# Attention with a threshold and a low-rank mixer on one core: the instruction order made by a list scheduler, u formed in row order, the threshold on ScalarE

## The chip, the core and the metric

The kernel runs on one core of a Trainium2 chip. The core has five instruction streams that run side by side and wait for each other by semaphores: TensorE (PE, matmuls and transposes, results to PSUM), VectorE (DVE), ScalarE (ACT), GpSimd (POOL, here the casts of weights and most of the DMA issues) and SyncE (SP, here the DMA transposes). Each takes its instructions strictly in the order in which the program lists them, so the order is part of the kernel. The metric is the device time of one execution in microseconds, lower is better. A "profile" is one execution taken by the hardware profiler, and its "span" reaches from the first to the last instruction.

## The reference

Eight batches of eight heads, sequence 576, head size 64. Attention keeps only the scores within tau = 0.02 of the row's maximum. Its output, 576 x 512 per batch, goes through a mixer: a low-rank mixing along the sequence (rank 32), a sum, and a two-layer network of width 2048. All inputs and the output are float32.

```python
scores = scale * np.matmul(q, k.transpose(0, 1, 3, 2))
thresh = np.max(scores, axis=-1, keepdims=True) - tau
scores = np.where(scores >= thresh, scores, -1000000000.0)
scores = scores - np.max(scores, axis=-1, keepdims=True)
attn = np.exp(scores)
attn = attn / (np.sum(attn, axis=-1, keepdims=True) + 1e-09)
x = np.matmul(attn, v)            # heads side by side: (batch, 576, 512)
xt = x.transpose(0, 2, 1)
h = xt @ U @ V
u = x + h.transpose(0, 2, 1)
ch = np.maximum(u @ w_ch1, 0.0) @ w_ch2
return (u + ch).astype(np.float32)
```

## The kernel before

Work is cut into 32 head pairs (`hp`, four to a batch `b`) and each pair into five score steps (`i`): four of 128 query rows with both heads apart (`x` = 0, 1), and a fifth of 64 rows that holds both heads in one tile. There are 160 steps and 288 score tiles of 128 x 576.

One step: TensorE forms the scores of a tile from `qT` and `kT` (lines 250 and 258, float32, into `scores`, which is held once). DVE copies them to `s_sb` with their sign turned and takes the row's minimum `m` (`weigh`, L267). ACT takes the exponential (`exponential`, L275). DVE adds tau to `m` (`threshold`, L282) and then zeroes what lies below the threshold and sums the row (`select`, L289, into one of eight `w_ring` buffers). SP transposes the weights by DMA into `wT` (L294, L297).

A pair's other work, in its order: its q and k are turned by TensorE (`prepare_qk`, L214 and two tails of 64 columns at L215) and copied by ACT with the scale on q (L222 to L231); v is split into two bf16 parts; the weights are multiplied with v (`mm`, L315, 40 matmuls) and copied out; the result is turned back to rows (`back`, L340 to L345) and divided by the row sums (`scale_rows`, L348, L353), which is x; a bf16 copy (`narrow`, L365) is multiplied with U (`low_rank`, L375) and gives `tt`, 32 rows. Then `turn` forms u transposed in one go: float32 transposes of x and, accumulated on them in the same PSUM bank, the product of `tt` and V (L390 to L395). ACT copies that to bf16 as `uT`.

When the fourth pair of a batch has its `uT`, its mixer units are put on a queue (`mixer_units`): 32 units of four matmuls with W1 and a relu (L415, L421), then units of eight matmuls with W2 (L437) for each 128 rows of output, the last of which adds the product of V and `tt` (L441, L445), since the output is u + ch and x alone is at hand in row order. DVE adds x (L450), POOL sends the rows (L454 to L458). The four loose PSUM banks are handed out by `bank1`.

The order is written out in one loop over pairs and steps. In pass `p` the scores of pair `p` run beside the preparation of pair `p + 1` (in step 1), the weighting of pair `p - 1` (step 2), its back and low rank (steps 3 and 4) and the turn of pair `p - 2` (step 0). Mixer units fill in by a fixed credit per step (`share`, L502). In the first six passes matmuls on a zero tile (`fill`, L470) keep TensorE's clock up. Weights are loaded by POOL, one piece a step from the second pair on.

Of the kernel before, what the change touches and what calls it, by code (L numbers as in the profile page):

```python
# [8 lines left out]
P = 128  # L9
# [7 lines left out]
DM = H * D  # L17
# [5 lines left out]
NPAIR = H // 2  # L23

# [5 lines left out]
def rows(i):  # L30
    return P if i < 4 else HB


@with_exitstack
def kernel(
# [22 lines left out]
    make_identity(nc, ident)  # L58

# [29 lines left out]
    ttpool = pool("tt", 4)  # L89
    upool = pool("uT", 2)  # L90
    opool = pool("o", 3)
# [7 lines left out]
    last = [0, 0, 0, 0]  # L99
    held = [False] * 4  # L100
    clock = [0]
    sums = []

    def bank1():

        while all(held):
            sums.pop(0)()
        n = min((n for n in range(4) if not held[n]), key=lambda n: last[n])
        held[n] = True
        return bank[n], n  # L110

    def free(*ns):

        for n in ns:
            clock[0] += 1
            last[n] = clock[0]
            held[n] = False

    def load_pair(src, b, hp, name, engine):
        raw = rawpool.tile([P, NT, 2, D], FP32, name=name, tag=name)  # L120
        sv = src[b, 2 * hp:2 * hp + 2].rearrange("j (p t) d -> p t j d", p=HB)
        for j in range(2):
            engine.dma_start(raw[0:HB, :, j, :], sv[:, 0:NT, j, :])  # L123
            engine.dma_start(raw[HB:P, 0:4, j, :], sv[:, NT:9, j, :])  # L124
        return raw

    def weight_units():

        def u():
# [5 lines left out]
        def vv():  # L135
# [8 lines left out]
        def w1(t, h):  # L144
# [3 lines left out]
        def w2(c):  # L148
# [4 lines left out]
        return ([u, vv] + [lambda t=t, h=h: w1(t, h) for h in range(2) for t in range(4)]  # L153
                + [lambda c=c: w2(c) for c in range(8)])

    def build_v(raw):

        vh = vpool.tile([P, NT, 2, 2, D], BF16, name="vh", tag="vh")
        for part, ts in ((P, slice(0, 4)), (HB, slice(4, 5))):
            src = raw[0:part, ts, :, :]  # L160
            hi = vh[0:part, ts, 0, :, :]
            nc.scalar.copy(out=hi, in_=src)  # L162
            nc.gpsimd.tensor_tensor(out=vh[0:part, ts, 1, :, :], in0=src, in1=hi,  # L163
                                    op=ALU.subtract)
        return vh

    ring = [0]

    class Batch:
# [3 lines left out]
        def __init__(self, b, before):  # L173
            self.b = b
            self.odd = b % 2
            self.h4 = slice(HB * self.odd, HB * self.odd + HB)

            self.main = slice(HB * self.odd, HB * self.odd + 512)
            self.rest = slice(0, HB) if self.odd else slice(512, S)
            self.even = before  # L180

        def start(self):

            self.x = xpool.tile([P, 4, DM], FP32, name="x", tag="x")
            self.tt = ttpool.tile([R, DM], BF16, name="tt", tag="tt")
            self.uT = upool.tile([P, 4, S], BF16, name="uT", tag="uT")
            if self.odd:
                self.x4 = self.even.x4
            else:
                self.x4 = x4pool.tile([P, DM], FP32, name="x4", tag="x4")  # L190

    class Pair:


        def __init__(self, b, hp):
            self.b, self.hp = b, hp

        def load(self, eq=None, ek=None):
            self.qraw = load_pair(q, self.b, self.hp, "qraw", eq or nc.gpsimd)
            self.kraw = load_pair(k, self.b, self.hp, "kraw", ek or nc.gpsimd)  # L200
            self.vraw = load_pair(v, self.b, self.hp, "vraw", nc.gpsimd)

        def prepare_qk(self):

            tails, t_ = bank1()
            copies = []
            out = []
            for x, raw in enumerate((self.qraw, self.kraw)):  # L210
                tT = qkpool.tile([P, S], FP32, name="qkT", tag="kT" if x else "qT")
                ps, n = bank1()
                for t in range(4):
                    nc.tensor.transpose(ps[:, t * P:(t + 1) * P], raw[:, t, :, :], ident)  # L214
                nc.tensor.transpose(tails[:, x * HB:(x + 1) * HB], raw[0:HB, 4, :, :],  # L215
                                    ident[0:HB, 0:HB])
                out.append(tT)
                copies.append((ps, n))
            self.qT, self.kT = out

            def q_main():
                nc.scalar.mul(out=out[0][:, 0:512], in_=copies[0][0], mul=-scale)  # L222
                free(copies[0][1])

            def k_main():
                nc.scalar.copy(out=out[1][:, 0:512], in_=copies[1][0])
                free(copies[1][1])

            def rest():
                nc.scalar.mul(out=out[0][:, 512:S], in_=tails[:, 0:HB], mul=-scale)  # L230
                nc.scalar.copy(out=out[1][:, 512:S], in_=tails[:, HB:P])  # L231
                free(t_)

            return q_main, k_main, rest

        def prepare_v(self):
            self.vh = build_v(self.vraw)

        def start(self):
            self.wT = wtpool.tile([P, NT, 2, S], BF16, name="wT", tag="wT")  # L240
            self.den = d_ring[(self.b * NPAIR + self.hp) % 4]

        def scores(self, i):

            if i < 4:
                sct = pair_bank
                for c in range(2):
                    for j in range(2):
                        hs = slice(64 * j, 64 * j + 64)
                        nc.tensor.matmul(sct[j][:, c, 0:HC], self.qT[hs, i * P:(i + 1) * P],  # L250
                                         self.kT[hs, c * HC:(c + 1) * HC], start=True, stop=True)
            else:
                one = pair_bank[0]
                sct = [one]
                for c in range(2):
                    for j in range(2):
                        hs = slice(64 * j, 64 * j + 64)
                        nc.tensor.matmul(one[hs, c, 0:HC], self.qT[hs, 512:S],  # L258
                                         self.kT[hs, c * HC:(c + 1) * HC], start=True, stop=True)
            self.sct = sct  # L260
            self.m = small.tile([P, 2], FP32, name="m", tag="m")
            self.ssb, self.esb = [], []

        def weigh(self, i, x):

            s_sb = spool.tile([P, S], FP32, name="s_sb", tag="s_sb")
            nc.vector.tensor_scalar(  # L267
                out=s_sb.rearrange("p (a c) -> p a c", a=2), in0=self.sct[x][:, :, 0:HC],
                scalar1=0.0, scalar2=None, op0=ALU.add, op1=ALU.min,
                accum_out=self.m[:, x:x + 1])  # L270
            self.ssb.append(s_sb)

        def exponential(self, x):
            e_sb = epool.tile([P, S], BF16, name="e_sb", tag="e_sb")
            nc.scalar.activation(out=e_sb, in_=self.ssb[x], func=ACT.Exp,  # L275
                                 bias=self.m[:, x:x + 1], scale=-1.0)
            self.esb.append(e_sb)

        def threshold(self):
            n = len(self.sct)  # L280
            self.thr = small.tile([P, 2], FP32, name="thr", tag="thr")
            nc.vector.tensor_scalar(out=self.thr[:, 0:n], in0=self.m[:, 0:n], scalar1=tau_f,  # L282
                                    scalar2=None, op0=ALU.add)

        def select(self, i, x):

            w_sb = w_ring[ring[0] % NW]
            ring[0] += 1
            nc.vector.scalar_tensor_tensor(  # L289
                out=w_sb[:, 0:S], in0=self.ssb[x], scalar=self.thr[:, x:x + 1],  # L290
# [324 lines left out]
```

## Time and profile before

| what | us |
|---|---|
| median of 3 runs | 752.41 |
| lowest and highest run | 750.87, 755.83 |
| the profiled execution's own time | 751.19 |
| its span | 749.4 |

The page of the profile gives the busy time of each engine, and a query by window gives the same for any stretch. A matmul's end is modelled and matmuls overlap in the array, so the lengths of matmuls that follow each other sum to more than the time they take; the starts are exact. In rows of groups, "idle before" is the engine's idle time just ahead of these instructions and what ended it. A DMA share of 1 means that the core's 16 DMA engines are busy all the time.

### The profile page before, as it was taken

The page shows a single profiled execution, that of the slowest core. Times are in us where ns is not written, and L with a number is a line of the kernel's source. Part 1 is how long each engine was busy: PE and PEld are TensorE (multiplying, and loading weights), DVE is VectorE, ACT ScalarE, POOL GpSimd, SP SyncE. Part 2 cuts the span into 40 slices and gives each one's busy share as a digit, 9 for nine tenths or more (in the row PEclk, how much of TensorE's full clock was granted, in tenths as well). Part 3 has the DMA queues.
Part 4 walks back from the last instruction along what each step waited for, and adds up shares of the span by engine and source line. Part 5 has one row for each costly group of instructions (what it writes and reads, how often), then busy time and mean ns, then how long its engine had stood idle before and what let it go on. Part 6 is the DMA issues. An engine that isn't in the chain of part 4 may idle for free.

```text
span 749.4 us, 15084 instructions
## 1 busy us (share of the span) xinstructions
PE 710.8 (95%) x5119; PEld 422.0 (56%) x5162; DVE 523.3 (70%) x1489; ACT 434.7 (58%) x961; POOL 380.2 (51%) x589
## 2 busy tenths in 40 slices
PE   9887789999999999999999999999999999999995
PEld 4454456665566555664566555665566555665562
DVE  4887487767977788667877778777877677778101
ACT  4565267755677455775577545774577555774340
POOL 9776555465655345554573456543664565310102
PEclk9998799999999999999999999999999999999998
DMA  6999997776974586766786686766886666545202
GB/s 123 165 136 185 158 183 133 109 116 109 178 133 99 107 132 150 121 106 102 136 150 109 116 149 119 132 98 103 147 146 114 115 140 124 100 75 85 52 15 56
DMA packets 220701, 90.30 MB, mean 120 GB/s; under 512 B 206208, under 2 KB 211264, under 8 KB 220624
## 3 DMA queue, kind: packets, MB, share of 16 engines
q1 hardware_dynamic: 195776, 47.52, 43.8%
q0 software_dynamic: 23632, 41.51, 26.8%
q8 instruction: 41, 0.67, 0.4%
q10 hardware_dynamic: 1216, 0.30, 0.2%
q14 instruction: 36, 0.29, 0.1%
HBM read 36.86 MB, written 9.44 MB: 62 GB/s over the span
## 4 chain that ended last, share of the span: by engine, by line
PE 77%; DVE 10%; ACT 5%; issue 3%; DMA 3%; POOL 1%; DVEq 0%; SPq 0%; POOLq 0%; ACTq 0%
PE bank L437 16%; PE scores L250 16%; PE bank L415 16%; PE bank L315 10%; DVE s_sb L267 5%; PE scores L258 4%; DVE w_ring L289 4%; PE bank L214 3%; ACT e_sb L275 3%; PE bank L390 2%; DMA wT<-w_ring 2%; PE bank L375 2%; PE bank L474 1%; PE bank L441 1%; PE bank L392 1%
## 5 line engine op out<-in xcount | busy, mean ns | idle before, releaser
L275 ACT ACTIVATE e_sb<-s_sb,m 128x576 bf16<-128x576 f32 x288 | 218.3, 775 | 131.3 <-DVE s_sb L267 87.5
L267 DVE TENSOR_SCALAR_CACHE_REDUCE s_sb<-scores 128x576 f32<-128x576 f32 x288 | 208.3, 748 | 103.8 <-PE scores L250 99.3
L289 DVE SCALAR_TENSOR_TENSOR w_ring<-s_sb,thr,e_sb 128x576 bf16<-128x576 f32 x288 | 230.9, 822 | 58.0 <-ACT e_sb L275 50.1
L250 PE MATMUL scores<-qkT 64*128 64x288 f32 x1024 | 167.7, 433 | 7.9 <-DVE s_sb L267 7.4
L163 POOL TENSOR_TENSOR vh<-vraw,vh 128x512 bf16<-128x512 f32 x64 | 55.7, 889 | 208.6 <-ACT vh L162 208.6
L415 PE MATMUL bank<-uT,W1b 128*128 128x288 bf16 x1024 | 145.8, 286 | 7.3 <-ACT R L421 6.8
L437 PE MATMUL bank<-W2b,R 128*128 128x512 bf16 x544 | 131.4, 380 | 3.4 <-issue 2.5
L250 PEld LDWEIGHTS scores<-qkT 64*128 64x128 f32 x1024 | 93.5, 187 | 53.4 <-issue 16.3
L415 PEld LDWEIGHTS <-W1b 128*128 128x128 bf16 x1024 | 94.0, 97 | 47.5 <-issue 21.4
L421 ACT ACTIVATE R<-bank 128x288 bf16<-128x288 f32 x256 | 97.3, 409 | 6.9 <-PE bank L415 1.4
L315 PE MATMUL bank<-wT,vh 128*64 128x288 bf16 (+1 forms) x1280 | 91.4, 292 | 5.8 <-DMA wT<-w_ring 5.6
L437 PEld LDWEIGHTS <-R 128*128 128x128 bf16 x576 | 51.7, 98 | 66.0 <-issue 12.0
L315 PEld LDWEIGHTS <-vh 128*64 128x64 bf16 (+1 forms) x1280 | 68.0, 111 | 32.0 <-issue 23.5
L398 ACT CAST uT<-bank 128x512 bf16<-128x512 f32 x32 | 18.7, 585 | 69.6 <-PE bank L392 69.6
L454 POOL DMA_DIRECT2D out_dram<-o x32 | 17.9, 558 | 72.7 <-DVE o L450 70.9
L450 DVE TENSOR_TENSOR o<-bank,x 128x512 f32<-128x512 f32 x36 | 24.8, 690 | 37.1 <-issue 21.2
L123 POOL DMA_DIRECT2D vraw<-in_v_dram x64 | 46.1, 721 | 2.7 <-issue 2.1
L222 ACT ACTIVATE qkT<-bank 128x512 f32<-128x512 f32 x32 | 19.1, 597 | 45.8 <-PE bank L214 45.8
L123 POOL DMA_DIRECT2D qraw<-in_q_dram x62 | 43.9, 707 | 3.4 <-issue 2.5
L123 POOL DMA_DIRECT2D kraw<-in_k_dram x62 | 43.9, 708 | 1.3 <-DMA W1b<-in_moe_w_ch_dram 0.8
L124 POOL DMA_DIRECT2D vraw<-in_v_dram x64 | 42.9, 671 | 1.2 <-DMA qraw<-in_q_dram 1.2
L124 POOL DMA_DIRECT2D kraw<-in_k_dram x62 | 40.9, 660 | 2.4 <-DMA W1b<-in_moe_w_ch_dram 2.4
(73 smaller groups left out, 701.7 us busy)
## 6 DMA issues: line engine op xcount, KB each, us to landing
out_dram<-o POOLq DMA_DIRECT2D x72, 128.0 KB, 3.0
vraw<-in_v_dram POOLq DMA_DIRECT2D x64, 80.0 KB, 4.0
wT<-w_ring SPq DMA_TRANSPOSE x320, 3.9
qraw<-in_q_dram POOLq DMA_DIRECT2D x62, 80.0 KB, 2.7
kraw<-in_k_dram POOLq DMA_DIRECT2D x62, 80.0 KB, 3.8
vraw<-in_v_dram POOLq DMA_DIRECT2D x64, 64.0 KB, 4.1
qraw<-in_q_dram POOLq DMA_DIRECT2D x62, 64.0 KB, 2.8
kraw<-in_k_dram POOLq DMA_DIRECT2D x62, 64.0 KB, 3.7
```

The source lines that it names most:

```text
L123: engine.dma_start(raw[0:HB, :, j, :], sv[:, 0:NT, j, :])
L124: engine.dma_start(raw[HB:P, 0:4, j, :], sv[:, NT:9, j, :])
L163: nc.gpsimd.tensor_tensor(out=vh[0:part, ts, 1, :, :], in0=src, in1=hi, op=ALU.subtract)
L250: nc.tensor.matmul(sct[j][:, c, 0:HC], self.qT[hs, i * P:(i + 1) * P], self.kT[hs, c * HC:(c + 1) * HC], start=True, stop=True)
L258: nc.tensor.matmul(one[hs, c, 0:HC], self.qT[hs, 512:S], self.kT[hs, c * HC:(c + 1) * HC], start=True, stop=True)
L267: nc.vector.tensor_scalar(out=s_sb.rearrange("p (a c) -> p a c", a=2), in0=self.sct[x][:, :, 0:HC], scalar1=0.0, scalar2=None, op0=ALU.add ...
L275: nc.scalar.activation(out=e_sb, in_=self.ssb[x], func=ACT.Exp, bias=self.m[:, x:x + 1], scale=-1.0)
L289: nc.vector.scalar_tensor_tensor(out=w_sb[:, 0:S], in0=self.ssb[x], scalar=self.thr[:, x:x + 1], in1=self.esb[x], op0=ALU.is_le, op1=ALU.mult,
L315: nc.tensor.matmul(self.av[c][64 * j:64 * j + 64, 0:HC], self.vh[0:nk, kt, part, j, :], self.wT[0:nk, kt, j, c * HC:(c + 1) * HC], start=( ...
L415: nc.tensor.matmul(ps[:, 0:HC], W1b[:, dt, ft * P:(ft + 1) * P], bt.uT[:, dt, c * HC:(c + 1) * HC], start=(dt == 0), stop=(dt == 3))
L421: nc.scalar.activation(out=R2[:, ft, lo:lo + HC], in_=ps[:, 0:HC], func=ACT.Relu)
L437: nc.tensor.matmul(ch, R2[:, ft, lo:lo + P], W2b[:, ft, :], start=(ft == 0), stop=False)
```

## The change

The loop is replaced by a list of tasks with a model. Every piece of work becomes a `Task`: an engine, an assumed cost, the tasks it depends on, the PSUM banks it takes or frees, and a rank. `Order.run` keeps a clock for each of the five engines and each bank. It repeatedly takes, for each engine, the tasks that could start within 0.15 us of the first that can, picks the lowest rank among them, and lists the earliest of the five picks. A task's end reaches other engines after a fixed delay (`SIGNAL`). Where the model sees TensorE idle for over 0.45 us, it lists fillers of 0.22 us. Mixer tasks have a due step (`when`): before it they rank last, from it on first. The 24 fillers at the very start stand outside of the model's clock.

```diff
+    SIGNAL = (0.25, 0.18, 0.15, 0.2, 0.1)
...
+        def rank(c):
+            s, t = c
+            if t.when is not None:
+                return (t.when - 1000.0 if t.when <= steps + (1.0 if t.kind == kind else 0.0) else t.when + 1000000.0, s)
+            return (t.ready + t.off, s)
...
+                first = min(s for s, _ in cands)
+                s, t = min((c for c in cands if c[0] <= first + 0.15), key=rank)
+                if best is None or s < best[0]:
+                    best = (s, t)
...
+                while at[PE] + 0.45 < s and last[n] <= at[PE]:
+                    self.filler(n)
+                    at[PE] += 0.22
...
+        due = NT * NPAIR * (b + 1) + 9
...
+                t = add(PE, 0.52, up, uT + weights1 + freed, banks=1, kind="p1",
+                        when=due + 10 * c + 10 * ft / 16)
...
+    for _ in range(24):
+        fill(0)
+    order.run()
```

The computation changes in four places. The threshold moves from DVE to ACT. q and k are loaded into one tile `qkraw`, so that their tails lie side by side and are turned by one transpose and copied once; the scale moves from the copy of q into `weigh`. The weighting is two tasks, one for each half of the columns, with the same 40 matmuls.

```diff
-            nc.vector.tensor_scalar(out=self.thr[:, 0:n], in0=self.m[:, 0:n], scalar1=tau_f,
-                                    scalar2=None, op0=ALU.add)
...
+            nc.scalar.activation(out=st["thr"][:, 0:nx], in_=st["m"][:, 0:nx], func=ACT.Identity,
+                                 bias=tau_t[:, 0:1], scale=1.0)
...
+            nc.tensor.transpose(bank[t.got[0]][:, 0:P], pr.qkraw[:, 4, :, :], ident)
```

And u is formed in row order. `spread` multiplies V and `tt` into rows, DVE adds that to x in place (`sum_u`), ACT makes a bf16 copy `ub`, and TensorE turns the copy in bf16. The tail rows of a batch are done once, with its last pair. The output then adds u from the tile, and the matmuls with V at the end of each output tile go.

```diff
-            for i in range(4):
-                nc.tensor.matmul(ups[:, i * P:(i + 1) * P], bt.x[:, i, cols], ident,
-                                 is_transpose=True, start=(i == 0), stop=False)
-            nc.tensor.matmul(ups, bt.tt[:, cols], Vb[:, 0:512], start=False, stop=True)
...
-                            nc.tensor.matmul(ch, Vb[:, i * P:(i + 1) * P], bt.tt, start=False,
-                                             stop=True)
...
+            for i in range(4):
+                nc.tensor.matmul(bank[t.got[0]][:, i * P:(i + 1) * P], Vb[:, i * P:(i + 1) * P],
+                                 bt.tt[:, pr.cols], start=True, stop=True)
+            if last:
+                nc.tensor.matmul(bank[t.got[1]][bt.h4, :], Vb[:, 512:S], bt.tt, start=True,
+                                 stop=True)
...
+            nc.vector.tensor_add(out=bt.x[:, :, pr.cols],
+                                 in0=bank[h.got[0]].rearrange("p (t m) -> p t m", t=4),
+                                 in1=bt.x[:, :, pr.cols])
...
+            nc.scalar.copy(out=pr.ub, in_=bt.x[:, :, pr.cols])
...
+            ps = bank[t.got[0]][:, 0:256].bitcast(BF16)
+            for i in range(4):
+                nc.tensor.transpose(ps[:, i * P:(i + 1) * P], pr.ub[:, i, :], identb)
```

Three places show how instructions now stand. The first is the start of TensorE's list. Before, 24 fillers (L474) stand ahead of the first transposes of q and k:

```order
L474 LDWEIGHTS idle
L474 MATMUL bank_143<-idle 128x512
L214 MATMUL bank_145<-ident,qraw 128x128 x4
L215 MATMUL bank_144<-ident,qraw 128x64
L214 MATMUL bank_146<-ident,kraw 128x128 x4
L215 MATMUL bank_144<-ident,kraw 128x64
L250 MATMUL scores_141<-qkT 128x288
```

Now the transposes are those of lines 311 and 326, and fillers (L215) stand on both sides of them:

```order
L215 LDWEIGHTS idle
L215 MATMUL bank_153<-idle 128x512
L311 MATMUL bank_153<-ident,qkraw 128x128 x4
L311 MATMUL bank_154<-ident,qkraw 128x128 x4
L326 MATMUL bank_155<-ident,qkraw 128x128
L215 LDWEIGHTS idle
L215 MATMUL bank_156<-idle 128x512
```

There are 49 fillers ahead of them now and four behind; in all 161, where there were 98. The first mixer matmul stands behind the 35th score step, where it stood behind the 27th.

The second place is the forming of u on TensorE in the steady part. Before, it stood in one piece between the scores of a pair's first step and the next mixer matmuls:

```order
L250 MATMUL scores_141<-qkT 128x288
L250 MATMUL scores_142<-qkT 128x288
L390 MATMUL bank_143<-ident,x 128x128 x4
L392 LDWEIGHTS tt
L392 MATMUL bank_143<-Vb,tt 128x512
L393 MATMUL bank_145<-ident,x_2447 128x64
L395 LDWEIGHTS tt
L395 MATMUL bank_145<-Vb,tt 128x64
L437 LDWEIGHTS R_147
```

Now the end of `spread` (L555) stands ahead of a fifth score step (L383); then comes the back of the next pair (L500, L504), and then the first of the four bf16 transposes (L590):

```order
L555 LDWEIGHTS Vb
L555 MATMUL bank_155<-tt,Vb 128x128
L383 MATMUL scores_151<-qkT 64x288 x4
L500 MATMUL bank_154<-ident,xT 128x128 x4
L504 MATMUL bank_156<-ident,xT 64x128
L590 LDWEIGHTS ub
L590 MATMUL bank_155<-identb,ub 128x128
```

The work is split in two, with DVE's sum and ACT's copy between the parts.

The third place is a score step in the middle of DVE's list. Before, the threshold stood between the two copies of scores and the two selects:

```order
L267 TENSOR_SCALAR s_sb,m<-scores_141 128x576
L267 TENSOR_SCALAR s_sb,m<-scores_142 128x576
L282 TENSOR_SCALAR thr<-m 128x2
L289 SCALAR_TENSOR_TENSOR w_ring_74,d_ring_88<-s_sb,thr,e_sb 128x576
L289 SCALAR_TENSOR_TENSOR w_ring_75,d_ring_88<-s_sb,thr,e_sb 128x576
```

Now DVE has the sum u (L566) there and no threshold:

```order
L396 TENSOR_SCALAR s_sb,m<-scores_151 128x576
L396 TENSOR_SCALAR s_sb,m<-scores_152 128x576
L566 TENSOR_TENSOR x<-bank_155,x 128x4x128
L423 SCALAR_TENSOR_TENSOR w_ring_82,d_ring_92<-s_sb,thr,e_sb 128x576
L423 SCALAR_TENSOR_TENSOR w_ring_83,d_ring_92<-s_sb,thr,e_sb 128x576
```

On ACT the threshold (L408) stands between the two exponentials of a step, among copies for other pairs and relus (L643):

```order
L531 CAST xb<-x_4627 64x128
L415 ACTIVATE e_sb<-s_sb,m 128x576
L408 ACTIVATE thr<-m,tau_t 128x2
L415 ACTIVATE e_sb<-s_sb,m 128x576
L643 ACTIVATE R_157<-bank_156 128x288
```

So a select, which had its threshold from its own engine, now has both its operands from ACT.

More of the change, by code (lines that the diff above doesn't have):

```diff
@@ L23, with __init__ @@
 NPAIR = H // 2
+NP = B * NPAIR
 def rows(i):
     return P if i < 4 else HB
+PE, VEC, SCA, POOL, SP = range(5)
+NEVER = float("inf")
+class Task:
+    __slots__ = ("engine", "cost", "fn", "deps", "off", "banks", "frees", "lag", "kind", "when",
+                 "left", "after", "ready", "end", "got")
+    def __init__(self, engine, cost, fn, deps=(), off=0.0, banks=0, frees=(), lag=0.0, kind=None,
+                 when=None):
+        self.engine, self.cost, self.fn = engine, cost, fn
+        self.deps = [d for d in deps if d is not None]
+        self.off, self.banks, self.frees, self.lag, self.kind = off, banks, frees, lag, kind
+        self.when = when
+        self.after, self.ready, self.end, self.got = [], 0.0, None, []
@@ L58 @@
     make_identity(nc, ident)
+    identb = consts.tile([P, P], BF16, name="identb")
+    nc.vector.tensor_copy(out=identb, in_=ident)
+    tau_t = consts.tile([P, 1], FP32, name="tau_t")
+    nc.vector.memset(tau_t, tau_f)
     wpool = pool("weights", 1)
@@ L127, in weight_units, with fill, got, head_rows @@
-    def weight_units():
-        def u():
+    def fill(n):
+        nc.tensor.matmul(bank[n], idle[:, 0:P], idle, start=True, stop=True)
+    order = Order(len(bank), fill)
+    add = order.add
+    done = {}
+    def got(*key):
+        return done.get(key)
+    def head_rows(src, b, hp):
+        return src[b, 2 * hp:2 * hp + 2].rearrange("j (p t) d -> p t j d", p=HB)
+    class Batch:
+        def __init__(self, b, before):
+            self.b = b
+            self.odd = b % 2
+            self.h4 = slice(HB * self.odd, HB * self.odd + HB)
+            self.rest = slice(0, HB) if self.odd else slice(512, S)
+            self.even = before
+        def start(self):
+            self.x = xpool.tile([P, 4, DM], FP32, name="x", tag="x")
+            self.tt = ttpool.tile([R, DM], BF16, name="tt", tag="tt")
+            if self.odd:
+                self.x4 = self.even.x4
+            else:
+                self.x4 = x4pool.tile([P, DM], FP32, name="x4", tag="x4")
@@ L151, in w2 @@
                 moe_w_ch2[2 * c * P:(2 * c + 2) * P, :].rearrange("(c p) m -> p c m", p=P))
[L153 to L190, printed above, removed]
@@ L465 @@
-    pairs = [Pair(b, hp) for b in range(B) for hp in range(NPAIR)]
-    NP = len(pairs)
-    mixq = []
-    loadq = weight_units()
-    def fill(n):
-        ps, m = bank1()
-        free(m)
-        for _ in range(n):
-            nc.tensor.matmul(ps, idle[:, 0:P], idle, start=True, stop=True)
-    credit = [0.0]
-    def mixer_pe():
-        cost, f = mixq.pop(0)
-        credit[0] -= cost
-        return f()
-    def mix(n):
-        while mixq and credit[0] > 0 and n > 0:
-            n -= 1
-            f, wait = mixer_pe()
-            if wait:
-                sums.append(f)
-            elif f:
-                f()
```

759 lines of the change are left out of this document (433 added, 326 removed).

## The prediction

> **What bounds the kernel now.** I read the page's busy shares and the chain that ended last first, then the busy time of each engine by stage, then TensorE's timeline through one step of the steady part and through the start. The columns of the second fence are: stretch, its length, busy us (instructions) of PE, PEld, DVE, ACT, POOL, then the granted clock, the DMA share and GB/s.
>
> ```profile
> PE 710.8 (95%) x5119; PEld 422.0 (56%) x5162; DVE 523.3 (70%) x1489; ACT 434.7 (58%) x961; POOL 380.2 (51%) x589
> PE 77%; DVE 10%; ACT 5%; issue 3%; DMA 3%; POOL 1%; DVEq 0%; SPq 0%; POOLq 0%; ACTq 0%
> ```
>
> ```profile
> 0.00:114.60 114.60, 96.87 (x597) 53.77 (x606) 81.16 (x246) 57.35 (x113) 78.41 (x123) 0.93 1.04 157
> 114.60:696.00 581.40, 570.25 (x4240) 342.78 (x4271) 436.25 (x1236) 361.67 (x809) 294.29 (x453) 1.00 0.70 121
> 696.00:741.40 45.40, 43.71 (x285) 25.43 (x285) 5.21 (x10) 15.69 (x39) 6.49 (x13) 1.00 0.19 41
> 741.40:749.40 8.00, 0.02 (x2) 0.00 (x0) 0.69 (x1) 0.00 (x0) 1.05 (x2) 0.74 0.15 33
> ```
>
> The program has three parts. Up to 114.6 us only attention runs, because the mixer of batch 0 needs all four of its head pairs. From 114.6 to 741.4 us TensorE is busy for 614 of 627 us at full clock, so there its work is the time. The last 8.0 us are the last output on its way. What the change is worth is therefore TensorE work removed after 114.6 us, plus or minus what it does to the start, where TensorE is not the limit: the DMA share there is 1.04, and what keeps PE "busy" is partly filler.
>
> **TensorE's work.** The next rows (start, length, engine, line, form, count) are one pair's items in the steady part. Because matmuls overlap, I price each item by the start of the next one, not by its length.
>
> ```profile
> 269.60 2.76 PE L315 MATMUL bank<-wT,vh 128*64 128x288 bf16 x40
> 272.29 1.24 PE L250 MATMUL scores<-qkT 64*128 64x288 f32 x8
> 275.20 0.60 PE L340 MATMUL bank<-ident,xT 128*128 128x128 f32 x4
> ...
> 275.84 1.19 PE L258 MATMUL scores<-qkT 64*64 64x288 f32 x8
> ...
> 278.79 0.39 PE L441 MATMUL bank<-tt,Vb 32*128 32x512 bf16 x1
> 279.11 0.55 PE L375 MATMUL bank<-xb,Ub 128*32 128x128 bf16 x5
> 279.59 1.90 PE L437 MATMUL bank<-W2b,R 128*128 128x512 bf16 x8
> 281.42 1.24 PE L250 MATMUL scores<-qkT 64*128 64x288 f32 x8
> 282.59 0.66 PE L390 MATMUL bank<-ident,x 128*128 128x128 f32 x4
> 283.18 0.39 PE L392 MATMUL bank<-Vb,tt 32*128 32x512 bf16 x1
> 283.50 0.27 PE L393 MATMUL bank<-ident,x 64*128 64x64 f32 x1
> 283.70 0.20 PE L395 MATMUL bank<-Vb,tt 32*128 32x64 bf16 x1
> 284.06 1.67 PE L437 MATMUL bank<-W2b,R 128*128 128x512 bf16 x7 [0.16 <-issue]
> 285.66 0.40 PE L445 MATMUL bank<-tt,Vb 32*64 32x512 bf16 x2
> 286.00 1.24 PE L250 MATMUL scores<-qkT 64*128 64x288 f32 x8
> 287.17 0.66 PE L214 MATMUL bank<-ident,qraw 128*128 128x128 f32 x4
> 287.75 0.27 PE L215 MATMUL bank<-ident,qraw 64*128 64x64 f32 x1
> 287.95 0.66 PE L214 MATMUL bank<-ident,kraw 128*128 128x128 f32 x4
> 288.54 0.27 PE L215 MATMUL bank<-ident,kraw 64*128 64x64 f32 x1
> 288.65 1.34 PE L250 MATMUL scores<-qkT 64*128 64x288 f32 x8
> 289.93 2.15 PE L315 MATMUL bank<-wT,vh 128*64 128x288 bf16 x32
> ```
>
> Removed. The old turn (L390 to L395) runs from 282.59 to 284.06 less 0.16 idle: 1.31 us, 32 times, 41.9 us. The matmul with V that ended each output tile (L441) takes 279.11 − 278.79 = 0.32 us, 32 times, 10.2 us; the double one (L445) 0.34 us, 4 times, 1.4 us. The two 64-wide tails (L215) take 0.20 + 0.11 us and become one transpose of 128 x 128, which by L214 costs 0.58 / 4 = 0.145 us: 0.165 us, 32 times, 5.3 us.
>
> Added. h takes four bf16 matmuls of 128 columns and the turn four bf16 transposes, eight per pair. Neither is in the trace. The nearest row is L375 (bf16, 128 columns): 0.48 / 5 = 0.096 us each. The low end is 2.69 / 40 = 0.067 us (L315), the high end an f32 transpose, 0.145 us. I take 0.098, since the form is nearly L375's with a wider weight: 32 x 8 x 0.098 = 25.1 us, bounds 17 and 37. The last pair of each batch adds one matmul of 512 columns (0.32) and four small transposes (0.10 each): 0.72 us, 8 times, 5.8 us. The net is −41.9 − 10.2 − 1.4 − 5.3 + 25.1 + 5.8 = **−27.9 us**, bounds −36 and −16. The Trainium skill (TensorE: Matmul & The Clock Gate, Back-to-back issue gap) gives about 81 ns for a sustained pair of weight load and 128-column matmul; by it the eight would come to 20.7 us and the sum would be 4.4 us lower. The same sentence gives 131 ns for 512 columns, which the trace denies: the eight of L437 before 281.42 took 229 ns each, so I keep the row. Scores, weighting, back, low rank and the mixer's other matmuls keep their forms and counts.
>
> **The other engines.** These are groups of the trace by line (busy us, mean ns | idle before).
>
> ```profile
> L289 DVE SCALAR_TENSOR_TENSOR w_ring<-s_sb,thr,e_sb 128x576 bf16<-128x576 f32 x288 | 230.9, 822 | 58.0 <-ACT e_sb L275 50.1
> L450 DVE TENSOR_TENSOR o<-bank,x 128x512 f32<-128x512 f32 x36 | 24.8, 690 | 37.1 <-issue 21.2 <-PE bank L441 12.7 <-PE bank L445 3.1
> L282 DVE TENSOR_SCALAR thr<-m 128x2 f32<-128x2 f32 x128 | 24.4, 191 | 4.4
> L365 ACT CAST xb<-x 128x512 bf16<-128x512 f32 x32 | 19.8, 617 | 9.3 <-DVE x L348 9.3
> L231 ACT COPY qkT<-bank 128x64 f32<-128x64 f32 x32 | 7.0, 220 | 0.0
> ```
>
> DVE loses the threshold (24.4 us, and up to 6 for 32 more of one column at 0.19 us or less) and gains the sum u: 40 adds in L450's form, 40 x 0.69 = 27.6 us. It stays at 522 us, 3.26 us per score step. ACT gains 160 thresholds of 0.22 us or less (35, by the small copies of L231) and 40 casts in L365's form (24.7), and loses 32 small copies (7.0): at most 487 us, 3.0 us per step. With about 4.2 us of TensorE's time per step (below) both have room, so I cost them at nothing; the cover is TensorE's mixer work. If that cover goes, DVE is late next. DMA and POOL work is the same in kind and number. Queued behind the new wait: on DVE a select now waits for ACT's threshold, and the next step's evacuation of scores stands behind it, with TensorE's next scores behind that.
>
> **The start.** The times on TensorE that I use:
>
> ```profile
> 10.05 1.24 PE L250 MATMUL scores<-qkT 64*128 64x288 f32 x8 [0.47 <-ACT qkT L226]
> 26.48 1.24 PE L250 MATMUL scores<-qkT 64*128 64x288 f32 x8 [1.07 <-DVE s_sb L267]
> 43.57 1.24 PE L250 MATMUL scores<-qkT 64*128 64x288 f32 x8 [1.16 <-DVE s_sb L267]
> 76.46 0.42 PE L315 MATMUL bank<-wT,vh 128*64 128x288 bf16 x1 [4.17 <-DMA wT<-w_ring]
> 112.64 0.60 PE L474 MATMUL bank<-idle 128*128 128x512 bf16 x2
> 113.08 0.60 PE L214 MATMUL bank<-ident,qraw 128*128 128x128 f32 x4
> 114.61 1.15 PE L415 MATMUL bank<-uT,W1b 128*128 128x288 bf16 x8
> ```
>
> Two things in the new order count against it. First, 49 fillers stand ahead of the first transposes where there were 24; at 0.22 us (113.08 − 112.64 for two) the 25 more move the first scores from 10.05 to 15.5 us. Second, the mixer begins behind the 35th score step, where it began behind the 27th. I reckon to the start of the 35th. For the pace I take 3.42 us a step, as in the second pair (26.48 to 43.57, five steps), and no DMA stall: 15.5 + 34 x 3.42 = 132 us. The fast end is 3.0 us a step, near the 2.9 us that the order itself puts into a step (76 us of work, below, and 108 fillers of 0.22 us, over 34): 117 us. The slow end adds the old stall of some 10 us around 76 us, where transposed weights landed late: 142 us, 145 with a slower pace.
>
> What TensorE has done by then pays part of it. Scores take 1.17 us a step (281.42 to 282.59), or 1.12 for the fifth of a pair, a weighting 2.69, q and k 1.3, back 0.64, low rank 0.48, h 0.4, the new turn 0.4 us. In the order 34 score steps, 8 preparations of q and k, 6 weightings, 5 of back, low rank and h and 4 turns stand there: 76 us, so 132 − 76 = 56 us are lost or filler. Before, 27 score steps, 6 preparations (of 1.48 us) and 4 of each of the rest are 61 us of 114.6: 54 us. The term is **+2 us**, bounds −13 and +15.
>
> **The steady part.** The windows leave TensorE 627 − 614 = 13 us of waits between 114.6 and 741.4 us. One of them is in the last pair's chain, which the new order covers with mixer work:
>
> ```profile
> 704.42 0.54 PE L375 MATMUL bank<-xb,Ub 128*32 128x128 bf16 x5 [1.32 <-ACT xb L365]
> ```
>
> The order places every item as soon as its model holds it ready, which saves idle but leaves no slack. I keep the 13 us, less this 1.3 us. Bounds: −8 and +25.
>
> **Sum.** 749.4 − 27.9 + 2 − 1.3 = 722.2 us of span. The run that was profiled took 751.19, 1.8 us more than its span, and the median of the runs is 1.2 us above that: 722.2 + 1.8 + 1.2 = **725 us**. Behind the last scores the order leaves 136 matmuls of 512 columns (0.229 us, 31 us), 184 of 288 (0.13 us in proportion, 24 us), 8 us of the last pairs' attention and the 8 us of output, so those scores stand at 651 us, and the 125 steps from 132 us on get (651 − 132) / 125 = 4.2 us each.
>
> **Rivals.**
> *The start is quicker and the model packs better*: first mixer work at 117 us (−15) and waits of 5 us (−8): about 702 us. For it: the order's own step of 2.9 us. Against it: the DMA share of 1.04 in the start. Chance 0.12.
> *The saved work comes back as waits, within 1%*: weighting waits for wT. In one pair of five or so the new order puts it two score steps behind the pair's last scores instead of three, about 10.9 us of TensorE work, where the old one left 289.93 − 275.84 = 14.1 us. An extra wait of 0.85 us per pair is 27 us and eats the whole saving: 752 us. For it: the trace has such a wait once (4.17 us). Against: it occurs only under the weights' loads. Chance 0.14.
> *Slower*: the threshold on ACT makes the round trip from DVE to ACT and back the clock of a step. DVE's 3.26 us a step plus the wait for exp and threshold must stay under TensorE's 4.2 us; from 0.9 us of wait on it decides. At 1.2 us a step takes 4.46 us, 0.29 more, 125 times: 725 + 36 = 761 us. For it: L289 already waits 50.1 us for ACT, and ACT stands in order behind its own copies. Against: that is 0.3 us a step. The Trainium skill (TensorE: Matmul & The Clock Gate, Architectural detail) says that ACT and DVE are strict FIFO queues, which is what would carry such a wait on; the trace does not deny it. Chance 0.12.
>
> **How the numbers follow.** The forecast has 0.62, its own range 706 to 744: prices −8 to +12, start −15 to +13, steady waits −8 to +25, seldom all on one side. To leave out no more than 2 in 10 I widen it to 703 and 750, part of the quick and of the 1% case included. About 1% is what a measurement of this kernel can tell from no change. Faster by over 1% (under 745) has 0.74, the forecast with its quick rival; within 1% 0.14; slower 0.12.
>
> **What would show it.** Right: TensorE over 95% busy from its first mixer matmul on, that one at 127 to 142 us, the first scores near 15.5 us, h and the turn at 0.7 to 0.9 us per pair, the granted clock at 1.00. Wrong: rows of weighting with idle time put down to wT in the steady part, idle time of scores put down to DVE and of select to ACT's threshold of over 0.7 us a step, or a first mixer matmul beyond 147 us.

## The result and the profile after

The changed kernel takes 718.3 us (median of 4 runs, 714.78 to 722.62) against 752.23 us: a ratio of 0.954, 95% interval 0.947 to 0.962. A second set of 6 runs gave 717.4 us and 0.951 (0.947 to 0.955). The forecast was 725 us, in a range of 703 to 750. The profiled execution took 720.96 us with a span of 719.2 us, against 751.19 and 749.4.

The page's line of busy times:

```profile
PE 686.6 (95%) x5225; PEld 416.6 (58%) x5225; DVE 514.9 (72%) x1371; ACT 480.1 (67%) x1105; POOL 377.2 (52%) x589
```

TensorE's share is the same 95%, which hides what happened. The windows show it, cut at the first mixer matmul (149.7 us now, 114.6 us before) and at the last matmul; columns as in the prediction:

```profile
0.00:149.70 149.70, 128.00 (x849) 70.88 (x850) 102.93 (x288) 81.71 (x175) 103.48 (x160) 0.91 1.08 151
149.70:711.20 561.50, 558.60 (x4378) 345.68 (x4376) 411.80 (x1084) 398.42 (x931) 272.71 (x428) 1.00 0.67 120
```

The same two stretches for the fillers alone (PE, PEld, DVE, then clock, DMA share and GB/s):

```profile
0.00:149.70 149.70, 40.58 (x157) 14.78 (x157) 0.27 (x1) 0.91 1.08 151
149.70:711.20 561.50, 1.19 (x4) 0.39 (x4) 0.00 (x0) 1.00 0.67 120
```

Read together with the windows of before, they split the 30.2 us of span into three parts. TensorE's work without fillers is 686.59 − 41.77 = 644.8 us, where it was 710.84 − 26.99 = 683.9 (the fillers' 26.99 are in the trace of before, 25.61 of them in its start): **−39.0**. Time of the start that is not such work is 149.7 − (128.00 − 40.58) = 62.3 us, where it was 114.6 − (96.87 − 25.61) = 43.3: **+18.9**. Behind the first mixer matmul, idle time and fillers are 561.5 − 558.6 + 1.2 = 4.1 us, where they were 12.8 + 1.4: **−10.1**. (Of the 12.8 us, 3.5 are matmuls that the trace of before does not show; what that changes is said with the steady waits below.) The last output takes 8.0 us in both.

So from 149.7 us on TensorE is busy for 99.5% of the time: there is hardly anything to gain in that part but by giving it less to do. What the change gave away lies ahead of it. These are the starts on TensorE that I read there:

```profile
15.95 1.24 PE L376 MATMUL scores<-qkT 64*128 64x288 f32 x8
...
66.91 1.24 PE L376 MATMUL scores<-qkT 64*128 64x288 f32 x8
...
72.93 0.40 PE L472 MATMUL bank<-wT,vh 128*64 128x288 bf16 x1 [4.46 <-DMA wT<-w_ring]
77.42 2.70 PE L472 MATMUL bank<-wT,vh 128*64 128x288 bf16 x19 [4.09 <-DMA wT<-w_ring]
...
87.28 0.42 PE L472 MATMUL bank<-wT,vh 128*64 128x288 bf16 x1 [5.64 <-DMA wT<-w_ring]
...
147.06 1.19 PE L383 MATMUL scores<-qkT 64*64 64x288 f32 x8
...
149.74 0.53 PE L633 MATMUL bank<-uT,W1b 128*128 128x288 bf16 x3
```

The first 17 steps take (66.91 − 15.95) / 17 = 3.00 us each, quicker than the 3.42 that the prediction used and as quick as its fast end. Then the two halves of one pair's weighting wait three times, 14.2 us in all, for transposed weights. Of this stretch, 60 to 90 us, the DMA issues are (KB each, median us to landing):

```profile
W1b<-in_moe_w_ch_dram POOLq DMA_DIRECT2D x4, 256.0 KB, 13.2
...
wT<-w_ring SPq DMA_TRANSPOSE x12, 11.6
```

Over the whole run a transpose lands in 3.9 us. Here it meets the weights' loads, and TensorE, which takes its list in order, waits with it.

### The profile page after: what moved, and what is told of

It is laid out like the page before. It is cut to its first block, busy times and chain, and to the rows that moved or that the text cites. A ratio compares the mean times of both kernels' runs of the same rounds, so it can differ in the third digit from the quotient of the medians.

```text
span 719.2 us, 15207 instructions
## 1 busy us (share of the span) xinstructions
PE 686.6 (95%) x5225; PEld 416.6 (58%) x5225; DVE 514.9 (72%) x1371; ACT 480.1 (67%) x1105; POOL 377.2 (52%) x589
## 5 line engine op out<-in xcount | busy, mean ns | idle before, releaser
L423 DVE SCALAR_TENSOR_TENSOR w_ring<-s_sb,thr,e_sb 128x576 bf16<-128x576 f32 x288 | 229.5, 827 | 53.3 <-ACT thr L408 27.9
L633 PE MATMUL bank<-uT,W1b 128*128 128x288 bf16 x1024 | 139.8, 287 | 1.9 <-DVE x L566 1.4
L643 ACT ACTIVATE R<-bank 128x288 bf16<-128x288 f32 x256 | 97.3, 403 | 51.6 <-PE bank L633 47.0
L472 PE MATMUL bank<-wT,vh 128*64 128x288 bf16 (+1 forms) x1280 | 101.3, 297 | 17.4 <-DMA wT<-w_ring 17.2
L268 POOL DMA_DIRECT2D qkraw<-in_q_dram x124 | 81.5, 670 | 56.0 <-PE bank L326 39.2
L472 PEld LDWEIGHTS <-vh 128*64 128x64 bf16 (+1 forms) x1280 | 63.8, 111 | 52.8 <-issue 43.4
L268 POOL DMA_DIRECT2D vraw<-in_v_dram x128 | 84.4, 673 | 14.1 <-POOL vh L349 7.1
L659 PEld LDWEIGHTS <-R 128*128 128x128 bf16 x576 | 53.3, 98 | 65.5 <-issue 11.6
L268 POOL DMA_DIRECT2D qkraw<-in_k_dram x124 | 80.4, 669 | 9.9 <-DMA W1b<-in_moe_w_ch_dram 4.9
L408 ACT ACTIVATE thr<-m,tau_t 128x2 f32<-128x2 f32 (+1 forms) x160 | 45.2, 283 | 14.3 <-DVE s_sb L396 14.1
L485 ACT COPY xT<-bank 128x288 f32<-128x288 f32 x64 | 24.3, 390 | 34.7 <-PE bank L472 34.4
L319 ACT COPY qkT<-bank 128x512 f32<-128x512 f32 x64 | 35.6, 579 | 11.1 <-PE bank L311 10.9
L215 PE MATMUL bank<-idle 128*128 128x512 bf16 x161 | 41.8, 398 | 1.2 <-DVE idle L175 1.2
```

The costliest lines, as they stand in the source:

```text
L215: nc.tensor.matmul(bank[n], idle[:, 0:P], idle, start=True, stop=True)
L268: queue.dma_start(raw[part, to, j, :], src[:, of, j, :])
L408: nc.scalar.activation(out=st["thr"][:, 0:nx], in_=st["m"][:, 0:nx], func=ACT.Identity, bias=tau_t[:, 0:1], scale=1.0)
L423: nc.vector.scalar_tensor_tensor(out=w_ring[r][:, 0:S], in0=st["s", x], scalar=st["thr"][:, x:x + 1], in1=st["e", x], op0=ALU.is_le, op1=A ...
L472: nc.tensor.matmul(av[64 * j:64 * j + 64, 0:HC], pr.vh[0:nk, kt, part, j, :], pr.wT[0:nk, kt, j, c * HC:(c + 1) * HC], start=(kt == 0 and ...
L633: nc.tensor.matmul(bank[t.got[0]][:, 0:HC], W1b[:, dt, ft * P:(ft + 1) * P], bt.uT[:, dt, c * HC:(c + 1) * HC], start=(dt == 0), stop=(dt ...
```

## The experiments

Every kernel was timed beside runs of the kernel before (752 to 753 us). The runs of the changed kernel scatter over 714 to 723 us, so differences of under 3 us between medians say little; the profiled executions are split as above.

**The old way of forming u in the listed order.** This takes the new u out and leaves the list, ScalarE's threshold and the shared tail of q and k.

```diff
-        h = done["h", p] = add(PE, 0.6 if last else 0.35, spread, [tt, weights0[1]], off=-3.0,
-                               banks=2 if last else 1, kind="h")
+        uT_ = done["uT_", p] = done["h", p] = add(PE, 1.31, turn, deps, off=-3.0, banks=2, kind="h")
...
+                    if g == 1:
+                        if i < 4:
+                            nc.tensor.matmul(ch, Vb[:, i * P:(i + 1) * P], bt.tt, start=False,
+                                             stop=True)
```

> The listed order with u formed in the old way (float32 turn, V's matmul at the end of each output tile, no sum on VectorE, no bf16 copy). If TensorE's work is the time and passes through one to one, the work that the new u saves comes back: 53.5 us (turn and V's matmuls) less 23.6 us (the new h and turns as the changed kernel's trace has them) is 30 us; this order happens to begin the mixer behind score step 28 instead of 35, worth 5 to 10 us; so 738 to 745 us, with TensorE idle under 5 us behind the first mixer matmul. Rival: the order alone made the gain, and the shorter u only turned into waits elsewhere: below 728 us.

It took 737.6 us, ratio 0.982 (0.978 to 0.986). Its two windows:

```profile
0.00:123.00 123.00, 105.40 (x660) 58.12 (x661) 77.30 (x226) 62.41 (x138) 87.36 (x137) 0.92 1.11 153
123.00:725.90 602.90, 600.91 (x4520) 363.63 (x4518) 414.29 (x1106) 399.27 (x953) 287.78 (x450) 1.00 0.67 118
```

TensorE is idle for 2.0 us of 602.9, so the short waits come from the list, not from the new u. With 37.55 us of fillers off, its work is 668.8 us: the new u saves 668.8 − 644.8 = 24.0 us, and the list with the shared tail 683.9 − 668.8 = 15.1 us. The work came back in the time, as the first theory said; at 737.6 us it falls just short of its 738. The profiled execution's span rose by less than the work, 14.7 us: the mixer begins behind the 28th step here, and the lost time of the start is 123.0 − (105.40 − 36.77) = 54.4 us instead of 62.3.

**The row sums first.** The copies that bring the fifth step's row sums to the other half of the partitions stand on POOL behind loads and weights. They get a better rank, and in the new list the first mixer matmul stands behind the 29th score step instead of the 35th.

```diff
-            done["den", p] = add(POOL, 1.1, sums, [done["den", p]], lag=2.5)
+            done["den", p] = add(POOL, 1.1, sums, [done["den", p]], off=-6.0, lag=2.5)
```

> The copies of row sums (POOL) rank ahead of loads and weights; the first mixer matmul then stands behind score step 29 instead of 35, all else alike. If the late start of the mixer is what the start costs, six steps at 3.9 us less the 14 us of attention work that moves behind it is some 9 us: 706 to 712 us, first mixer matmul at 118 to 130 us. Rival: the start is bound by its DMA volume whatever the order, and the mixer would only wait for weights or for DMA there: 716 to 720 us.

The first mixer matmul came at 124.8 us, as expected, and the start's lost time in the profiled execution fell from 62.3 to 51.6 us. But the median is 715.2 us (713.2 to 719.2), only 2 to 3 us less, and not within the 706 to 712 expected. The earlier start of the mixer is there; why so little of it reaches the time is not shown by this run.

**Without the first 24 fillers.** They stand ahead of the list and outside of the model's clock, which lists 25 more for the same wait.

```diff
-    for _ in range(24):
-        fill(0)
     order.run()
```

> The changed kernel without the 24 fillers ahead of the listed order, all else alike. If the shift of the first scores (15.95 us instead of 10.05) passes through, 5 to 6 us less: about 713 us. Rival: the DMA stalls between 68 and 88 us absorb it, since weights and transposes then meet earlier: 717 to 719 us.

It took 714.5 us (711.7 to 718.3), 3 to 4 us less. The first scores came at 11.26 us instead of 15.95, so by the medians most of the shift passes through, though 3 to 4 us are hardly more than the scatter. The stall is still there: weightings wait 16.1 us for `wT`, where they wait 17.2 in the changed kernel. The result lies between the theories, nearer to the first.

**The threshold back on VectorE.**

```diff
-            nc.scalar.activation(out=st["thr"][:, 0:nx], in_=st["m"][:, 0:nx], func=ACT.Identity,
-                                 bias=tau_t[:, 0:1], scale=1.0)
+            nc.vector.tensor_scalar(out=st["thr"][:, 0:nx], in0=st["m"][:, 0:nx], scalar1=tau_f,
+                                    scalar2=None, op0=ALU.add)
...
-        thr = add(SCA, 0.2, threshold, mins, off=-7.0)
+        thr = add(VEC, 0.1, threshold, mins, off=-7.0)
```

> The threshold back on VectorE in the listed order, all else alike; the order happens to begin the mixer behind score step 32 instead of 35. If ScalarE's threshold is hidden, nothing but that start: 713 to 719 us, with TensorE's idle time behind the first mixer matmul as before, 3 us. Rival: the wait of select for ScalarE's threshold (27.9 us in all) holds the steps: below 710 us, and TensorE less idle.

It took 715.5 us (711.7 to 721.6), within the scatter of the changed kernel. The wait of select by the groups of the trace, first the changed kernel, then this one:

```profile
L423 DVE SCALAR_TENSOR_TENSOR w_ring<-s_sb,thr,e_sb 128x576 bf16<-128x576 f32 x288 | 229.5, 827 | 53.3 <-ACT thr L408 27.9 <-ACT e_sb L415 13.7 <-DMA wT<-w_ring 10.4
```

```profile
L423 DVE SCALAR_TENSOR_TENSOR w_ring<-s_sb,thr,e_sb 128x576 bf16<-128x576 f32 x288 | 228.4, 820 | 24.0 <-ACT e_sb L415 9.4 <-DMA wT<-w_ring 6.5 <-DVE thr L408 0.9
```

ScalarE's threshold makes select wait 27.9 us in all, 0.17 us a step, and taking that wait away buys nothing clear of the scatter: VectorE was not the limit. TensorE is idle for 3.4 us behind the first mixer matmul, as expected. Where the threshold runs does not matter here.

**The changed kernel once more**, beside the three that follow.

> The changed kernel once more, beside the three that follow: 714 to 723 us.

717.4 us, 713.8 to 720.9. Its first mixer matmul stands at 149.1 us and its weightings wait 16.2 us for `wT` ahead of it, so the start described above is no chance of one execution.

**The weights' loads left out.** W1 and W2 are set to a constant on VectorE, so 8 MB of reads and the casts on their way are gone; the mixer's matmuls run on that constant. TensorE's list is the changed kernel's.

> The changed kernel with W1 and W2 not loaded but set to a constant on the chip, so their 8 MB of reads are left out; order on TensorE unchanged. If the weights' loads make the start's stall, no weighting waits over 1 us for wT, the pace falls from 3.86 to about 3.3 us a step, the first mixer matmul comes at 128 to 134 us instead of 149.7, and the time is 699 to 706 us. Rival: attention alone fills the DMA engines in the start: first mixer matmul beyond 143 us and 712 us or more.

It took 698.1 us, with runs from 697.5 to 700.0 us, a third of the scatter of the six runs beside it. No weighting waits for DMA any more. The first scores, the 35th step's scores and the first mixer matmul on TensorE:

```profile
15.41 1.24 PE L378 MATMUL scores<-qkT 64*128 64x288 f32 x8
...
124.81 1.19 PE L385 MATMUL scores<-qkT 64*64 64x288 f32 x8
...
127.48 0.65 PE L635 MATMUL bank<-uT,W1b 128*128 128x288 bf16 x4
```

That is (124.81 − 15.41) / 34 = 3.22 us a step, and 22 us earlier than the 147.06 of the changed kernel. The stall, its cost of 19 to 20 us, and most of the scatter of the runs come from the weights' loads.

Two other causes can be looked for in the same traces. The mixer now runs on a constant (0.01 here, 0 in the next experiment), which might change the granted clock; but behind the first mixer matmul the clock is 1.00 with and without the loads, and that part is not shorter (562.7 us, 561.5 with the loads). POOL no longer issues the 16 loads; but the transposes are issued by SP, and between 60 and 90 us they land in 4.0 us instead of 11.6. Setting the constant also costs something: it keeps VectorE busy until 18.3 us, and the fifth step's scores come at 30.4 us instead of 27.2, so the loads cost, if anything, more than the 19 to 20 us.

**The same with the kernel before.**

> The kernel before with W1 and W2 not loaded but set to a constant on the chip, all else alike, to set beside the changed kernel without these loads, which fell by 19 to 20 us. If the loads cost the kernel before only its own stall of some 10 us around 76 us: 739 to 744 us, and the changed kernel's order makes the same loads dearer. Rival: they cost both the same: 731 to 735 us.

It took 738.3 us (737.8 to 739.7), 14 us less. This lies between the theories, nearer to the first: the same loads cost the new order some 5 to 6 us more than the old one, though with the scatter of the loaded runs that difference is rough. (Here the constant is set by 9.7 us, ahead of the first scores, and delays nothing.) Without them the two kernels differ by 738.3 − 698.1 = 40 us, with them by 35.

**Row sums first, and the weights one piece in two steps.**

```diff
             t = gate[n] = add(POOL, cost, fn, [], off=2.0, lag=4.0)
             to.append(t)
-            n += 1
+            n += 1 if n < 8 else 2
```

> The copies of row sums first, and the pieces of W1 and W2 loaded one in two score steps from the ninth on instead of one a step; the order on TensorE stays that of the row-sums version. If the waits of weighting for wT before the first mixer matmul come from the weights' loads meeting the transposes, those waits fall from 11 us to under 4, and the time by 6 to 10 us: 705 to 709 us. Rival: the DMA engines are short in the start as a whole, so that the same waits come later or elsewhere: 713 to 717 us.

717.2 us, from 710.2 to 720.3 (a sixth run took 721.7): no gain. In the profiled execution (710.2 us, the best one) the waits for `wT` ahead of the first mixer matmul did fall to 2.9 us, as expected, and that matmul came at 111.2 us. But then the core stalls later. The windows from 105 and from 120 us:

```profile
105.00:120.00 15.00, 14.04 (x121) 8.86 (x121) 12.36 (x35) 11.80 (x28) 10.71 (x15) 1.00 1.21 163
120.00:140.00 20.00, 14.17 (x104) 9.40 (x105) 11.95 (x34) 10.87 (x26) 13.57 (x21) 0.83 0.84 149
```

TensorE is idle for 5.8 of the 20 us from 120 us on, with one wait of 5.8 us of scores for VectorE, and the clock falls to 0.83. What VectorE waits for stands in the rows of POOL, VectorE and TensorE there:

```profile
124.94 0.59 POOL L455 DMA_DIRECT2D d_ring<-d_ring  x1
130.19 0.54 POOL L456 DMA_DIRECT2D d_ring<-d_ring  x1 [4.67 <-DMA d_ring<-d_ring]
...
131.92 0.17 DVE L491 TENSOR_SCALAR rec<-d_ring 128x10 f32<-128x10 f32 x1 [7.46 <-DMA d_ring<-d_ring]
...
134.51 2.96 PE L376 MATMUL scores<-qkT 64*128 64x288 f32 x8 [5.83 <-DVE s_sb L396]
```

In every second batch the row sums need two copies, and the second overwrites what the first reads. So POOL waits until the first has landed, VectorE waits for the second with the reciprocal of the sums (L491), and the next scores wait for VectorE. The first copy is slow to land while weights are loaded, but the DMA engines are not short all along: from 128.8 to 131.8 us they move next to nothing, since POOL issues no loads and VectorE hands on no weights to transpose. By its time the result is the rival's, and the waits do come elsewhere; that the DMA engines are short in the start as a whole is not shown. Why the runs that were not profiled took 4 to 11 us more is not known.

**Row sums first, without the first fillers**, and the same with the spaced weights.

> The copies of row sums first and no 24 fillers at the start, with the weights loaded one piece a score step as in the changed kernel. If the two edits add up (7 us by the profiled spans of the one, 8 by the other, 3 to 4 each by medians): 707 to 712 us, and what the spaced loads add to that is under 3 us. Rival: without the spaced loads the DMA stall gives back what the earlier start wins: 713 to 716 us.

710.5 us (704.5 to 714.4), ratio 0.944 (0.940 to 0.949). The two edits add up to about 7 us.

> The same without the 24 fillers at the very start. If starting 4.7 us sooner passes through once the DMA stall is smaller: 4 to 5 us below the version with them. Rival: the DMA engines absorb it: within 2 us of it.

708.2 us (706.3 to 710.9), ratio 0.939 (0.936 to 0.943): better than both kernels, by 9 us than the changed one. Against the version with fillers it is 9 us less, more than the 4 to 5 expected, though the first scores come only 4.7 us sooner. The late stall is here too (scores wait 5.5 us for VectorE at 133 us). Why the spaced loads scatter so widely with the fillers and not without them was not found; against the version with unspaced loads it is 2.3 us, which the scatter covers.

## Why the prediction was right, and where its terms were wrong

**What bounds the kernel: right.** Behind the first mixer matmul the time is TensorE's work. With the old u the time rose by 19 to 20 us and TensorE stayed busy to within 2.0 us.

**The work term: right for u, too small elsewhere.** It was put at −27.9 us and measured −39.0. The part of u was −22.6 of the 27.9, and the old-u run gives −24.0. Items of one pair in the steady part of the changed kernel:

```profile
409.80 0.39 PE L555 MATMUL bank<-tt,Vb 32*128 32x128 bf16 x4
410.12 1.19 PE L383 MATMUL scores<-qkT 64*64 64x288 f32 x8
...
411.85 0.39 PE L590 MATMUL bank<-identb,ub 128*128 128x128 bf16 x4
412.18 1.24 PE L376 MATMUL scores<-qkT 64*128 64x288 f32 x8
...
414.83 0.60 PE L311 MATMUL bank<-ident,qkraw 128*128 128x128 f32 x4
415.37 1.26 PE L376 MATMUL scores<-qkT 64*128 64x288 f32 x8
...
418.30 0.60 PE L311 MATMUL bank<-ident,qkraw 128*128 128x128 f32 x4
418.73 0.27 PE L326 MATMUL bank<-ident,qkraw 128*128 128x128 f32 x1
418.94 0.55 PE L540 MATMUL bank<-xb,Ub 128*32 128x128 bf16 x5
```

h takes 0.32 and the turn 0.33 us: 0.081 us for each of the eight, where 0.098 was assumed from L375. The Trainium skill's 81 ns (TensorE: Matmul & The Clock Gate, Back-to-back issue gap), which the prediction set beside its own price, agrees with this row. The undersized piece is the rest, 5.3 us foreseen and 15.1 measured. Of it, q and k with their tail take 0.54 + 0.43 + 0.21 = 1.18 us per pair where 1.48 stood and 1.315 was foreseen, 9.6 us in all. The remaining 5 us (some 8 with the matmuls that the trace of before does not show) lie in instructions that did not change, for which the prediction had kept the old prices. Most of it is the 1024 matmuls with W1. Priced by the start of the next instruction, without the idle time that the profile counts, they take 137.6 us behind the first of them before, 130.0 now and 130.7 in the old-u run, so it is the list that makes them cheaper. Two causes can be read from the traces. Before, TensorE stood idle 14 times, 6.8 us in all, until a relu on ScalarE freed a bank for them, and the first 0.16 us of such a wait lie under the modelled end of the matmul ahead and count as work; now there is no such wait. And a run of them was followed by scores 52 times, now 10 times: 12 then take 1.58 us (at 137.99 us before), where 12 ahead of W2's matmuls take 1.48 (at 406.50 us now). No run tries the two apart.

**The other engines cost nothing: right.** VectorE 514.9 and ScalarE 480.1 us against 522 and at most 487. One price was short: the threshold takes 0.283 us on ScalarE, 45.2 us in all, where at most 35 was put. The threshold's wait exists and is hidden, which the run with the threshold on VectorE shows.

**The start: the step that failed.** It was put at +2 us and measured +19. The first half of it held: the 25 extra fillers moved the first scores to 15.95 us (15.5 foreseen), and the pace ahead of the stall is 3.0 us (3.42 foreseen), 3.2 over all 34 steps without the loads. The choice to leave out the stall was wrong, although the row with the old stall of 4.17 us was quoted and the DMA share of 1.04 was read: it went to the slow end of the range (145 us for the 35th step) instead of into the sum, and 147 us is what came. The run without the weights' loads has the 35th step at 125 us, so 22 us there are theirs, of which the forecast's slow pace hid 7. The first mixer matmul at 149.7 us is also beyond the 147 us that the prediction itself had named as a sign of being wrong; its other signs came out right, but for h and the turn, which at 0.65 us per pair are even below the 0.7 to 0.9 named. The prediction treated the mixer's late place in the list as given; the row-sums run shows that six of the eight steps came from one rank on POOL.

**The steady waits: wrong side.** 11.7 of 13 us were kept, and 2.9 remain, or 4.1 with fillers. The old-u run, with 2.0 us idle, shows that the list does this. The prediction took "no slack" as a risk; listing by this model left 0.5% idle.

**A reading of the trace of before that was off.** The page of before counts 544 matmuls of L437 beside 576 weight loads: 32 are missing from the trace, and where they stood it shows idle time put down to "issue", 2.5 us in all. The run of the kernel before without the loads has all 576, no such idle time and otherwise the same waits, 9.3 us instead of 12.8. So some 3 of the −10.1 us above belong to the work term: about −42 for the work and −7 for the waits. In the prediction's rows the matmul behind 283.70 is one of the missing ones (its weight load stands at 283.83), so the old turn takes 1.24 us, not 1.31, and the term of u was 2.2 us too large by this.

The errors in the terms of work and of steady waits, −11.1 and −8.8 us, and the one in the start, +17, nearly cancel: that the forecast of 725 us is only 7 us off is in part luck. **The rivals:** the quick one was half right (waits fell by 10 us, the start did not get quicker); the wait of weighting for wT in the steady part did not occur, as all 17.2 us of such waits lie ahead of 128 us, under the loads or just behind them; select's wait for ScalarE, 27.9 us for the threshold and 13.7 for the exponential, is 0.26 us a step, far from the 0.9 at which it would decide. (By the prediction's own 4.15 us a step, that rival's 0.29 us is 0.31, and its time 764 us.)

## What to carry to other kernels

When one engine is busy all through the steady part, split the time at the moment from which this holds, and judge a change separately on both sides: here 39 us of work and 10 us of steady waits were gained and 19 us given away in the start, where the page's 95% showed neither. Check the counts first: a matmul that is missing from a trace looks like a wait. An order made by a model is only as good as its ranks for the small tasks that gate a long chain, and its clock must include everything that the program runs before the list. In a start where the DMA share is over 1, a stall that the trace of before shows belongs in the sum until a run has shown that the new order removes it.

## What was not expected of the hardware

The weights' loads, 8 MB of reads with a cast to bf16, cost 14 us in the kernel before and 19 to 20 us in the changed one, although they are issued over more than 60 us (from 48 to 112 us in the changed kernel). From 60 to 90 us a DMA transpose lands in 11.6 us instead of 4.0 without the loads, and in the kernel before in 8.3 instead of 4.4. They also make most of the scatter: ten runs of the changed kernel lie within 9 us, and the four without loads within 2.4. And during a stall the granted clock falls, here to 0.83 over 20 us: the scores at 134.51 us, behind the wait, take 2.89 us to the next instruction, where 1.17 is usual. The changed kernel's work ahead of its first mixer matmul takes 87.4 us at a clock of 0.91, and without the loads 81.0 us at 0.99. So a stall costs more than its wait.
